# A two-layer attention and MLP backward on one Trainium2 core: dV stored in two halves, and two zero stores moved from the w1 backward to the dW1 chunks

## The chip, the core and the metric

The kernel runs on one core of one Trainium2 chip. The metric is the device time of one execution in microseconds (us), lower is better. A core has five engines that run their own instruction streams: PE (matrix products; "PEld" is the loading of its stationary operand), DVE (vector), ACT (scalar), POOL and SP. SP does nothing here but issue DMA transfers, in program order; POOL issues some as well. All transfers share the core's 16 DMA engines.

## The reference, cut to what matters

One token x of width 1024 goes through four residual layers: attention A, MLP B, then A and B again, with the same weights both times. The kernel returns the output and the gradients of everything.

```python
def _A_ref(x, k_cache, v_cache, wq, wo):        # 32 query heads, 4 kv heads, last W = 4096 keys
    q = (x @ wq) ...; p = softmax(q k^T * Dh**-0.5); o = p v
    return o @ wo
def _B_ref(x, w1, b1, w2):                       # F = 3584
    h = x @ w1 + b1;  act = h * tanh(softplus(h));  return act @ w2

x = x + A(layernorm(x));  x = x + B(layernorm(x))
x = x + A(layernorm(x));  x = x + B(layernorm(x))
...
out, vjp = jax.vjp(f, A_x, A_k_cache, A_v_cache, A_wq, A_wo, B_w1, B_b1, B_w2)
return (out, *vjp(grad_out))
```

The caches are 32768 keys long and only the last 4096 are used. So the gradients dK and dV (4 x 32768 x 128 in bf16, 33.5 MB each) are zero in seven eighths of their rows. These zeros have to be written too: 112 stores of 512 KB (the kernel calls them zero jobs), each from one zeroed tile `zt`. The last eighth of dK and of dV, 4 MB each, and the weight gradients dWq, dWo (8 MB each), dW1, dW2 (7 MB each) are sums of a few outer products and are computed at the end.

## The kernel before, in words

**The order of the work.** Attention forward (A1), MLP forward (B2), attention forward (A3), a pass that does the last MLP forward and backward at once (B4), attention backward of A3, a pass over w2 that finishes B4 forward and serves the backward of B2, the w1 backward of B2 (L798), attention backward of A1 (L817), and then the tail: all large gradients. The schedule is manual: each engine's instructions run in the order in which the Python code issues them.

**The zero stores** are used as filling for the DMA queues. `bg_zeros(n, after)` (L134) lets POOL copy one column of a tile `after`, so that POOL waits until that tile is there (a gate), and then POOL issues n zero stores. `zeros(n)` (L128) lets SP issue n of them, with no gate. The table `Z` (L1158) says how many go where: 85 go by POOL and 27 by SP.

**The w1 backward** (L788 to L815) streams w1 in 16 loads of 448 KB (L366) through a pool of six tiles. For each chunk, PE transposes 14 blocks (L196), DVE or ACT copies them back into the same tile (L146, L149), and PE does 14 small products with `dh` (L232). The load of a chunk is issued by SP when the products of the chunk six before it have freed its tile. `Z["W1m"]`, the tuple (2, 5, 8, 11, 13) in the kernel before, names the chunks at which a zero store is issued by POOL, gated on the chunk before (L793).

**The tail** is a list of jobs (L1288 to L1297), run one after the other. A job makes one chunk of a gradient: PE writes outer products into two PSUM tiles, ACT and DVE cast them to bf16 into an SBUF tile ("evacuation", `evac`, L143, which gives each piece to the engine with less work so far), and SP stores the chunk. The list is:

- 14 chunks of dW2, then 8 chunks of dW1 (`dw_tall` L1069, `dw_wide` L1084; stores at L1080 and L1099);
- 8 further chunks of dW1, each followed by one of the 8 chunks of dV (`dkv`, L1105);
- 16 chunks of dWo;
- 16 half chunks of dWq and 8 chunks of dK, two and one in turn (dWq is stored at L1101, every second half chunk, 1 MB).

The chunks of dW1, dW2 and dWo go to a ring of staging tiles: six in `wo_b`, six `st_o`, four in `V`, sixteen in `wq_b`. dWq goes to `wq_b` at fixed places. dV and later dK are gathered in the tile `K`, whose old contents are no longer needed. `late_prep` puts small preparations between the jobs, and after it `zeros(2)` is inserted into the list at positions 27 and 33 (L1294), which is among the dW1 and dV chunks. Zero jobs that are left at the end would be issued last (L1297); none are.

**The stores of dV and dK** are in `dkv`:

```python
if j % 4 == 3 and (j > 4 or half):
    hs = slice(4 * j - 12 if half else 0, 4 * j + 4)
    for g in range(G):
        nc.sync.dma_start(ov[:, g, hs, :], st[:, g, hs, :])
```

With `half` false, nothing is stored until the eighth chunk (j = 7), and then four stores of 1 MB go out, one for each kv head g. Chunk j fills the rows 4j to 4j+3 of each partition and head, so the first four chunks fill rows 0 to 15 and the others rows 16 to 31.

Of the kernel before, what the change touches and what calls it, by code (L numbers as in the profile page):

```python
# [23 lines left out]
def kernel(  # L24
# [40 lines left out]
    NW2 = TF // 2  # L65
# [62 lines left out]
    def zeros(n):  # L128
        for _ in range(min(n, len(zero_jobs))):
            nc.sync.dma_start(zero_jobs.pop(0), zt[:])  # L130
# [3 lines left out]
    def bg_zeros(n, after):  # L134

        if n:
            nc.gpsimd.tensor_copy(gate_t[:], after[:, 0:1])
        for _ in range(min(n, len(zero_jobs))):
            nc.gpsimd.dma_start(zero_jobs.pop(0), zt[:])  # L139
# [91 lines left out]
    def mm(out_ap, lhsT, rhs, start, stop, **kw):  # L231
        nc.tensor.matmul(out_ap, lhsT=lhsT, rhs=rhs, start=start, stop=stop, skip_group_check=True, **kw)  # L232
# [117 lines left out]
    def wo_load(c):  # L350
        if c < NR:
            w = wo_kept[c]
        else:
            w = strm.tile([P, 2, D], BF16, name="wo_c", tag="st")[:]
        nc.sync.dma_start(w, wo_v[c])
        return w
# [38 lines left out]
    area = {}  # L395
# [44 lines left out]
    def attn_fwd(x_col, lname, first):  # L440
# [30 lines left out]
        if not first:  # L471
            for c in range(NR, min(NO, NR + NB)):
                held[c] = wo_load(c)
            bg_zeros(Z["A3"], n_bf)
            for w in wq_t:
# [193 lines left out]
    def mlp_fwd(x_col, lname, g_bf):  # L669
# [5 lines left out]
        for i in range(2 * TD):  # L675
            t, hf = i // 2, i % 2
            w = w1_load(i)
            if i == 0:
                bg_zeros(Z["B2a"], x_col)
            if i == 4:  # L680
# [17 lines left out]
        sv["dact"] = dact  # L698
        x_new, wg = w2.rest(0, g_bf, x_col, f"x_{lname}", gbc, Z["B2"], last)
        return x_new, sv, wg  # L700
# [5 lines left out]
    def w1_block(b, hh):  # L706
        w = strm.tile([P, HT, CB], BF16, name="w1_b", tag="st")
        nc.sync.dma_start(w[:], w1_v[:, hh * HT:(hh + 1) * HT, b * CB:(b + 1) * CB])
        return w

    def mlp_turn(x_col, lname, wg, g_col, nxt):
# [22 lines left out]
        def lo0(b):  # L734
            return max(b - 1, 0) * FB

        def X(b, hh):
            wf = ws[b][hh][:].rearrange("p t f -> p (t f)")
            for k in range(2):
                xpose(*alt_blocks(wf[:, k * 1024:(k + 1) * 1024], 4), None, True)  # L740

        for b in range(NBK):
            if b:
                bg_zeros(Z["B4"][b], dh_bf[:, lo0(b):])
            ws[b] = [w1_block(b, hh) for hh in range(2)]
# [9 lines left out]
            if not b:  # L755
                bg_zeros(Z["B4"][b], m["y"])
            X(b, 0)
# [30 lines left out]
    def w1_T():  # L788
# [3 lines left out]
        ws[i] = w  # L792
        if i in Z["W1m"]:  # L793
            bg_zeros(1, ws[i - 1])
# [254 lines left out]
    def ev_out(out_ap, in_ap, f=1.0):  # L1049
        evac(out_ap, in_ap, 1.22 * f, 1.05 * f)  # L1050
# [10 lines left out]
    def out_banks():  # L1061

        if "pair" in pools:
            ts = [pools["pair"].tile([P, 1024], FP32, name="ops", tag="pair") for _ in range(2)]
            return [t[:, k * 512:(k + 1) * 512] for t in ts for k in range(2)], [(0, 2, ts[0][:]), (2, 2, ts[1][:])]
        bs = [psum1([P, 512], FP32, "ops") for _ in range(4)]
        return bs, [(k, 1, bs[k]) for k in range(4)]
# [37 lines left out]
    def dkv(x3, y3, x1, y1, out_t, half):  # L1105
        ov = out_t[0, :, Sk - W:, :].rearrange("g (p t) d -> p g t d", p=P)

        def chunk(j):
            st = kv["K"]
            bs, gs = out_banks()  # L1110
            for lay, (x, y) in enumerate(((x3, y3), (x1, y1))):
                for c in range(NC):
                    mm(bs[c], x[32 * c:32 * c + 32, j * P:(j + 1) * P],
                       y[32 * c:32 * c + 32, :, :].rearrange("p g d -> p (g d)"), lay == 0, lay == 1, tile_position=(32 * c, 0))
            for k, n, ap in gs:
                t0 = 4 * j + k
                ev_out(st[:, :, t0:t0 + n, :].rearrange("p g t d -> p t g d"), ap.rearrange("p (t g d) -> p t g d", t=n, g=G), n / 2)
# [5 lines that stand above are left out]
        jobs.extend([lambda j=j: chunk(j) for j in range(TJ)])  # L1123
# [31 lines left out]
        for _ in range(min(n, len(prep))):  # L1155
            prep.pop(0)()

    Z = dict(B2a=1, B2={0: 1, 4: 1, NW2 - 2: 3}, A3=14, B4=[2, 2, 2, 2, 2, 2, 5], A3c=6, A3d=28, B4w={1: 1, 4: 1, 7: 1, 10: 1, 12: 2}, W1=0, W1m=(2, 5, 8, 11, 13), A1c=3, A1d=23)  # L1158


    x1 = None
# [35 lines left out]
    x1, sA1 = attn_fwd(x0, "A1", True)  # L1197
# [51 lines left out]
    def r3(nm):  # L1249
        return area[nm].rearrange("p (g d) -> p g d", g=G)  # L1250
# [4 lines left out]
    def take(nm):  # L1255
        stage[nm] = jobs[:]
        del jobs[:]

    take("w")
    dkv(area["p3"], r3("do3"), sA1["p"], r3("do1"), out_3, False)  # L1260
    take("v")
    dw_tall("wo", HQ, out_5.rearrange("(c p t) d -> c p t d", p=P, t=2))
    take("o")
# [27 lines left out]
    weave(stage["q"], stage["k"], 2)  # L1291
    for at, f in zip((8, 11, 24, 27, 30, 40, 43, 46, 49, 51, 53), late_prep):
        jobs.insert(at, f)
    for at in (27, 33):  # L1294
        jobs.insert(at, lambda: zeros(2))
    run(1000)
    zeros(1000)  # L1297
# [31 lines left out]
```

## Time and profile before

| | |
|---|---|
| median of 11 runs | 444.97 us (440.87 to 448.15) |
| the profiled execution | 443.3 us, of which its span (first to last instruction) is 441.5 us |
| busy share of the span | PE 72%, ACT 50%, DVE 55%, POOL 15% |
| moved by DMA | 171.18 MB, 388 GB/s over the span |
| zero stores | 85 by POOL, 27 by SP, 512 KB each |
| w1 backward | about 262 to 290 us of the span |
| attention backward of A1 | about 290 to 326 us |
| tail | 326 us to the end |

How to read the profile: the page cuts the span into 40 equal slices and gives the busy share of each engine in tenths, the granted PE clock in tenths of full speed, the mean busy share of the 16 DMA engines, and the GB/s that they moved. A view by stretches gives the same for any stretch of time. A timeline lists instructions in order of time, and in square brackets how long the engine was idle just before and what ended that. A DMA has an issue time and a landing time; the view of DMA issues gives the time between the two.

### The profile page before, as it was taken

Reading aid. Unit: us, or ns where it says so; the run is one execution under the profiler, and the core shown is the slowest. Engines: PE = TensorE matmul, PEld = TensorE weight load, DVE = VectorE, ACT = ScalarE, POOL = GpSimd, SP = SyncE. Lnnn points to the kernel's source line nnn. Section 1 sums busy time; section 2 is a strip of 40 time slices with the busy share of each in tenths; the row PEclk is TensorE's granted clock in tenths of the full one; section 3 lists DMA queues with packets and bytes.
Section 4 is the critical chain, followed back from the end, with each engine's and each line's share of the span. In section 5 each row is a group of like instructions: output and inputs, shape, how many; then the busy total and the mean of one; then the engine's idle time right before and its main releaser. Section 6 shows DMA issues by size and latency. Waiting matters only on the chain.

```text
span 441.5 us, 11711 instructions
## 1 busy us (share of the span) xinstructions
PE 319.9 (72%) x5004; PEld 215.1 (49%) x5004; DVE 241.0 (55%) x494; ACT 219.3 (50%) x254; POOL 64.7 (15%) x168
## 2 busy tenths in 40 slices
PE   1565855597989989887995677787957588688830
PEld 0343525486376989875974676765421122211100
DVE  3134201196343766673547545464369889899930
ACT  1123100075143877867844333426047888798940
POOL 2000000011320322322333011214010010000000
PEclk9989555585888999999999559969965555555555
DMA  8999999999999999999999999999999986999997
GB/s 316 427 416 417 407 408 389 408 366 359 379 416 363 366 371 372 392 406 416 415 410 380 411 368 351 405 415 415 418 393 408 405 323 269 371 404 406 421 422 303
DMA packets 48720, 171.18 MB, mean 388 GB/s; under 512 B 4928, under 2 KB 12124, under 8 KB 44572
## 3 DMA queue, kind: packets, MB, share of 16 engines
q1 hardware_dynamic: 36208, 125.58, 72.3%
q0 software_dynamic: 12416, 44.84, 25.7%
q8 instruction: 39, 0.64, 0.6%
q14 instruction: 13, 0.11, 0.1%
q10 hardware_dynamic: 44, 0.01, 0.0%
HBM read 71.58 MB, written 98.84 MB: 386 GB/s over the span
## 4 chain that ended last, share of the span: by engine, by line
PE 24%; ACT 13%; DMA 11%; DVE 4%; issue 2%; POOL 1%; ACTq 0%; DVEq 0%; SPq 0%
DMA w_c<-in_B_w_dram 8%; PE tps L196 6%; PE ops L232 6%; PE acc L232 5%; ACT wq_b L149 3%; ACT K L149 3%; DMA out_dram<-wq_b 2%; ACT st_o L149 2%; PE sm L232 2%; ACT V L149 2%; ACT wo_b L149 2%; PE rw L995 1%; PE wps L155 1%; PE d L232 1%; PE tps L629 1%
## 5 line engine op out<-in xcount | busy, mean ns | idle before, releaser
L139 POOL DMA_DIRECT2D out_dram<-zt x85 | 45.8, 542 | 45.0 <-DMA out_dram<-zt 38.8
L232 PEld LDWEIGHTS <-w_c 128*128 128x128 bf16 x1120 | 37.4, 102 | 29.4 <-DMA w_c<-in_B_w_dram 23.2
L639 ACT COPY w_c<-tps 128x1024 bf16<-128x1024 bf16 x28 | 28.3, 1012 | 33.7 <-PE tps L629 26.3
L653 DVE CUSTOM_DVE_ANT_0 scr<-w_c,gbc 128x1024 bf16<-128x1024 bf16 x28 | 34.2, 1221 | 16.0 <-DMA w_c<-in_B_w_dram 14.8
L232 PE MATMUL ops<-V 2*128 2x512 bf16 (+1 forms) x160 | 33.4, 602 | 4.8 <-ACT V L149 1.2
L149 ACT CAST wq_b<-ops 128x1024 bf16<-128x1024 f32 (+1 forms) x33 | 35.9, 1128 | 1.9 <-PE ops L232 1.8
L146 DVE CAST wq_b<-ops 128x1024 bf16<-128x1024 f32 (+1 forms) x31 | 34.4, 1138 | 2.0 <-PE ops L232 1.8
L149 ACT COPY K<-tps 128x1024 bf16<-128x1024 bf16 x20 | 19.5, 1032 | 29.1 <-PE tps L196 29.0
L232 PEld LDWEIGHTS <-V 128*128 128x128 bf16 (+2 forms) x448 | 16.8, 102 | 33.7 <-issue 32.0
L232 PE MATMUL ops<-wo_b 2*128 2x512 bf16 x120 | 24.0, 569 | 9.8 <-ACT wq_b L149 2.7
L232 PE MATMUL acc<-a_pair,w_c 128*128 128x16 bf16 x448 | 15.9, 173 | 13.7 <-DMA w_c<-in_B_w_dram 13.7
L629 PE MATMUL tps<-ident_bf,w_c 128*128 128x128 bf16 x224 | 23.5, 270 | 0.7 <-DMA w_c<-in_B_w_dram 0.7
L149 ACT COPY w_b<-tps 128x1024 bf16<-128x1024 bf16 x20 | 19.5, 1015 | 5.3 <-PE tps L196 5.2
L232 PE MATMUL q<-wq_b,nA_pair 128*32 128x512 bf16 x128 | 10.6, 455 | 15.3 <-DMA wq_b<-in_A_wq_dram 15.3
L146 DVE COPY K<-tps 128x1024 bf16<-128x1024 bf16 x12 | 8.1, 690 | 24.0 <-PE tps L196 24.0
L248 DVE COPY yr<-acc 128x512 f32<-128x512 f32 x6 | 4.2, 692 | 30.9 <-PE acc L232 30.9
L232 PEld LDWEIGHTS <-wo_b 2*128 2x128 bf16 (+1 forms) x184 | 7.6, 101 | 27.2 <-issue 24.9
L146 DVE COPY w_c<-tps 128x1024 bf16<-128x1024 bf16 (+1 forms) x20 | 12.7, 650 | 14.2 <-PE tps L196 11.9
L149 ACT CAST K<-ops 128x1024 bf16<-128x1024 f32 x17 | 17.1, 1012 | 6.3 <-PE ops L232 5.5
L196 PE MATMUL tps<-ident_bf,K 128*128 128x128 bf16 x256 | 20.1, 240 | 0.2 <-ACT K L149 0.2
L146 DVE CAST K<-ops 128x1024 bf16<-128x1024 f32 x15 | 18.3, 1221 | 3.1 <-PE ops L232 2.7
L196 PE MATMUL tps<-ident_bf,w_c 128*128 128x128 bf16 x224 | 16.6, 231 | 4.7 <-DMA w_c<-in_B_w_dram 4.6
(326 smaller groups left out, 657.2 us busy)
## 6 DMA issues: line engine op xcount, KB each, us to landing
out_dram<-zt POOLq DMA_DIRECT2D x85, 512.0 KB, 10.4
w_c<-in_B_w_dram SPq DMA_DIRECT2D x32, 448.0 KB, 6.4
w_c<-in_B_w_dram SPq DMA_DIRECT2D x28, 512.0 KB, 8.5
out_dram<-zt SPq DMA_DIRECT2D x27, 512.0 KB, 10.6
wo_c<-in_A_wo_dram SPq DMA_DIRECT2D x24, 512.0 KB, 7.8
wq_b<-in_A_wq_dram SPq DMA_DIRECT2D x8, 1024.0 KB, 21.3
out_dram<-K SPq DMA_DIRECT2D x8, 1024.0 KB, 9.6
out_dram<-wq_b SPq DMA_DIRECT2D x8, 1024.0 KB, 10.3
```

Source lines behind the costliest of these rows:

```text
L139: nc.gpsimd.dma_start(zero_jobs.pop(0), zt[:])
L146: nc.vector.tensor_copy(out_ap, in_ap)
L149: nc.scalar.copy(out_ap, in_ap)
L155: nc.tensor.matmul(ps, lhsT=ident_bf[:], rhs=ident_bf[:, None, :].to_broadcast([P, 4, P]), start=True, stop=True, skip_group_check=True)
L196: nc.tensor.transpose(ps[:, b, :], ap, ident_bf[:])
L232: nc.tensor.matmul(out_ap, lhsT=lhsT, rhs=rhs, start=start, stop=stop, skip_group_check=True, **kw)
L248: nc.vector.tensor_copy(yr[:], bank[:])
L629: nc.tensor.transpose(self.ps[c][:, b, :], w[:, 1, b * P:(b + 1) * P], ident_bf[:])
L639: nc.scalar.copy(self.w[c][:, 1, :], self.ps.pop(c)[:].rearrange("p b c -> p (b c)"))
L653: nc.vector.tensor_tensor_reduce(out=scr[:], in0=w[:, 0, :], in1=gbc[:], scale=1.0, scalar=0.0, op0=ALU.mult, op1=ALU.add, accum_out=self. ...
L995: nc.tensor.transpose(ps[:, j, :], sp[:, j, :], ident_bf[:])
```

## The change

```diff
-    Z = dict(..., W1m=(2, 5, 8, 11, 13), ...)
+    Z = dict(..., W1m=(2, 8, 13), ...)
...
-    dkv(area["p3"], r3("do3"), sA1["p"], r3("do1"), out_3, False)
+    dkv(area["p3"], r3("do3"), sA1["p"], r3("do1"), out_3, True)
...
-    for at in (27, 33):
+    for at in (24, 27, 33):
         jobs.insert(at, lambda: zeros(2))
```

Three things are edited. The two zero stores at chunks 5 and 11 of the w1 backward, with their gates, are gone from POOL's program. A third pair of zero stores stands in SP's program among the dW1 chunks, so there are six in place of four; of the 14 dW1 stores from `wq_b`, the pairs now follow the 6th, the 7th and the 8th, where before they followed the 7th and the 9th. And dV is stored in two halves: four stores of 512 KB (16 rows of 256 bytes for each partition and head) after its fourth chunk, and four after its eighth; dK is stored as before. In SP's program the first half of dV follows the 10th of the 14 dW1 stores from `wq_b`, and the second half the 14th.

The number of zero stores stays 112: 83 by POOL and 29 by SP. The bytes moved are the same.

More of the change, by code (lines that the diff above doesn't have):

```diff
@@ L1156, in nextprep @@
             prep.pop(0)()
-    Z = dict(B2a=1, B2={0: 1, 4: 1, NW2 - 2: 3}, A3=14, B4=[2, 2, 2, 2, 2, 2, 5], A3c=6, A3d=28, B4w={1: 1, 4: 1, 7: 1, 10: 1, 12: 2}, W1=0, W1m=(2, 5, 8, 11, 13), A1c=3, A1d=23)
+    Z = dict(B2a=1, B2={0: 1, 4: 1, NW2 - 2: 3}, A3=14, B4=[2, 2, 2, 2, 2, 2, 5], A3c=6, A3d=28, B4w={1: 1, 4: 1, 7: 1, 10: 1, 12: 2}, W1=0, W1m=(2, 8, 13), A1c=3, A1d=23)
     x1 = None
```

## The prediction

> **What bounds the kernel now.** I read the page's slices first, then the view by stretches, then SP's timeline and its landing times for the end, and PE's and POOL's timelines for the w1 backward. From the page, the DMA share of the 40 slices and what was moved:
>
> ```profile
> DMA  8999999999999999999999999999999986999997
> GB/s 316 427 416 417 407 408 389 408 366 359 379 416 363 366 371 372 392 406 416 415 410 380 411 368 351 405 415 415 418 393 408 405 323 269 371 404 406 421 422 303
> ```
>
> The DMA engines are full in nearly every slice; the exceptions are the first, two slices around 353 to 375 us, and the last. No engine is full over the span (PE 72%). So time is to be won where DMA has a hole that later bytes could fill, or where bytes stand ahead of something that an engine waits for. The view by stretches, for the tail (start:end, its length, busy us of PE, PEld, DVE, ACT, POOL, PE clock, DMA share, GB/s):
>
> ```profile
> 328.00:356.00 28.00, 18.42 (x106) 4.41 (x104) 25.50 (x30) 23.09 (x23) 0.59 (x4) 0.50 1.01 401
> 356.00:364.00 8.00, 7.57 (x54) 2.59 (x49) 6.37 (x7) 7.15 (x7) 1.12 (x6) 0.50 0.75 294
> 364.00:380.00 16.00, 12.95 (x89) 4.29 (x83) 15.30 (x21) 13.76 (x14) 0.00 (x0) 0.50 0.71 287
> 380.00:402.00 22.00, 15.95 (x88) 3.69 (x89) 20.02 (x23) 18.94 (x21) 1.02 (x2) 0.50 1.01 405
> 402.00:425.00 23.00, 18.63 (x102) 4.02 (x95) 20.52 (x18) 19.93 (x22) 0.00 (x0) 0.50 1.02 416
> 425.00:441.50 16.50, 0.00 (x0) 0.00 (x0) 0.00 (x0) 0.28 (x1) 0.00 (x0) 0.50 0.83 345
> ```
>
> To see: the hole is 8 x 0.25 = 2.0 us and 16 x 0.29 = 4.6 us, 6.6 us in all. Through it and to 425 us DVE and ACT stay about 90% busy with the evacuations, and in their lists of waits no DMA stands: they wait for PE alone, shortly. So the tail has two clocks. The chain of evacuations runs from 326.6 to 425.3 us and sets when the last store, dK, can go; DMA sets what follows. SP's timeline of the tail, and the landing times of the last two kinds of store (issue to landing, us, the last number):
>
> ```profile
> 347.68 8.39 SPq L1099 DMA_DIRECT2D out_dram<-wq_b  x7
> 356.12 1.11 SPq L130 DMA_DIRECT2D out_dram<-zt  x2
> 360.04 2.80 SPq L1099 DMA_DIRECT2D out_dram<-wq_b  x2
> 362.89 1.11 SPq L130 DMA_DIRECT2D out_dram<-zt  x2
> 364.53 10.43 SPq L1099 DMA_DIRECT2D out_dram<-wq_b  x5
> 376.75 3.05 SPq L1121 DMA_DIRECT2D out_dram<-K  x4
> 425.31 4.20 SPq L1121 DMA_DIRECT2D out_dram<-K  x4
> ...
> out_dram<-wq_b SPq DMA_DIRECT2D x1, 1024.0 KB, 6.7
> out_dram<-K SPq DMA_DIRECT2D x4, 1024.0 KB, 9.6
> ```
>
> To see: the 4 MB of dV come at 376.75, after the hole. Its first store found the queue empty and landed in 3.9 us. The last store of dWq, of the same size, was issued at 423.76 and took 6.7 us: 2.8 us of other bytes were still ahead of it. For the w1 backward, PE's timeline, and after the "..." POOL's:
>
> ```profile
> 273.62 0.96 PE L196 MATMUL tps<-ident_bf,w_c 128*128 128x128 bf16 x14 [1.71 <-DMA w_c<-in_B_w_dram]
> 277.72 0.96 PE L196 MATMUL tps<-ident_bf,w_c 128*128 128x128 bf16 x14 [0.54 <-DMA w_c<-in_B_w_dram]
> 284.08 0.96 PE L196 MATMUL tps<-ident_bf,w_c 128*128 128x128 bf16 x14 [0.97 <-DMA w_c<-in_B_w_dram]
> 287.40 0.96 PE L196 MATMUL tps<-ident_bf,w_c 128*128 128x128 bf16 x14 [0.78 <-DMA w_c<-in_B_w_dram]
> ...
> 271.48 0.53 POOL L139 DMA_DIRECT2D out_dram<-zt  x1 [0.28 <-issue]
> 281.39 0.53 POOL L139 DMA_DIRECT2D out_dram<-zt  x1 [0.28 <-issue]
> ```
>
> To see: PE waits here for loads of w1, and the two zero stores shown, which compete with them, are the two that go.
>
> **Part 1, two zero stores less in the w1 backward.** Chunks that don't wait follow each other by 1.13 to 1.15 us. From chunk 6 (273.62) to chunk 15 (287.40) there are nine steps in 13.8 us, where 9 x 1.15 = 10.3 us would do: 3.4 us could go at most. By bytes: 1 MB at the 390 GB/s of 272 to 288 us is 2.7 us. The store of 271.48 lay wholly ahead of the last load, 1.35 us. That of 281.39 landed about 7.7 us later (the landing time of zero stores there), at 289.1, so some four fifths of it was served before 287.4: 1.1 us. Against this 2.4 us, the store of chunk 13 stays, and since chunk 13 is now reached sooner, it is issued sooner beside the same last loads. The price lies between 0 (the loads wait for their tiles, not for DMA) and 2.7 us; I take 1.9, near the upper end, since the waits name the loads and DMA is full. POOL's two gates and issues (0.19 and 0.53 us each) go as well, worth nothing: POOL stood idle 4.2 and 3.3 us before these gates.
>
> What follows is late by nothing new: from the layer norm at 290 us to the start of the tail at 326.6 the chain of waits names PE, DVE, ACT and POOL and no DMA, and the 23 zero stores that SP issues there wait only for each other. So 1.9 us earlier at 290 is 1.9 us earlier at 425.
>
> The DMA page of the Trainium skill ("DMA: Bandwidth & Descriptors", section "Queues, rings and completion order") says that each DMA engine takes turns between the queues that have work, a packet at a time. By that rule a zero store on POOL's queue takes every other turn from the loads until it is done, so both stores would have cost their full share, 2.7 us, where I take 1.9.
>
> **Part 2, two zero stores more in the tail.** 1 MB, 2.5 us of DMA at 416 GB/s. The pairs now stand after the stores issued at 354.01, 355.74 and 360.04, just before the first part of the hole (2.0 us, from 356 on). They fill it and leave 0.5 us. If part 1 brings less than its 2.7 us of DMA time, the hole is wider by the difference, relative to the evacuations, since DMA comes to it with less work. SP pays two issues of about 0.5 us, at a place where it waits up to 2.7 us for the next evacuation. In the scheduled program each DMA that SP issues waits for the landing of its eighth predecessor; eight of 512 KB are 10 us, and landings here take 2.4 to 5.6 us, so this stops nobody.
>
> **Part 3, dV in two halves.** The fourth dV chunk is evacuated by 365.9 us (DVE's cast of 364.67, 1.23 us), so 2 MB, 5.0 us, are issued from about 366 on, over a hole of 4.6 us. They leave 0.4 us. This adds a wait: SP holds for that evacuation. Behind it stand the last four dW1 stores (366.87 us and later), late by one or two us at most, and their tiles are next written by dWq after 397 us. Two more waits change: chunks 1 and 5 of dK now wait for the first and the second half of dV, where the first waited for all. dV's last 1 MB landed at 389.9 (378.57 + 11.3), the first dK cast is at 399.3: 9 us of cover. In the scheduled program the casts of dV's chunks 5 to 8, which write `K` while the first half is read from it, wait for PE alone. Four more DMAs are issued, 0.4 to 0.6 us of SP each, beside its waits. Rows of 4 KB in place of 8 KB: the zero stores have rows of 4 KB too, and 308 to 324 us, nothing but zero stores nearly, moved 414 to 423 GB/s, as the 1 MB stores of dK did (421). So nothing.
>
> Here the same page (section "Bandwidth") speaks against the change: transfers should be batched to 1 MiB or more. By its fit (section "Anatomy of one DMA", 2.0 us fixed for each transfer issued by POOL), an estimate for four more is up to 8 us if nothing overlapped. The queued 512 KB stores at 414 to 423 GB/s show that here it does.
>
> **The sum.** DMA is relieved by 6.6 of hole less 2.5 of zeros, 4.1 us, more than the 2.8 us of backlog at the last dWq store. So at 423.76 the queue is empty, and the evacuations bound the end. Then only dWq's last 1 MB and dK's 4 MB are to move after 425 us: 5.24 MB, where 16.5 us x 345 GB/s = 5.69 MB moved before. 0.45 MB at 421 GB/s is 1.1 us. By landings, the last dWq store would land 2.8 us earlier, but dK's first store can't land before 425.31 + 3.9 = 429.2 and its fourth, 2.5 us for each, before 436.7, against 439.0 (428.2 + 10.8): at most 2.3 us. I take 1.3, nearer the count of bytes. So 1.9 + 1.3 = 3.2 us. The profiled execution took 443.3 us (span 441.5, and 1.8 around it): 440.1. The median of the runs is 1.7 above that execution, so of a median **445.0 - 3.2 = 441.8 us**. About 0.5%, 2.2 us, is what a measurement of this kernel can tell from no change.
>
> **Rivals.**
> - *Only one of the two gains.* For it: the zeros of 266.3 and 283.8 us stay, and the largest PE wait (1.71 us at 273.62) comes from a load issued at 267.4, before the first removed store could disturb it. Or the tail's backlog is smaller in other executions than in this one. Against: DMA is full through the stretch, and the 6.7 us landing is plain. 445.0 less 1.3 to 1.9: about 443.4.
> - *The edit is hidden.* w1's loads run at the rate at which PE frees tiles, and the end is set by the evacuations and dK's own 10 us, so nothing moves: 445.0. Against it speak the nine steps of 13.8 us. The half store not acting at all is excluded by the scheduled program.
> - *Slower: the moved megabyte is paid at the end.* Place: the hole. If the two zeros bring nothing in the w1 backward, and the hole is already filled (the evacuations come later or DMA comes with more backlog, as the 40 slices can't exclude for other executions), then 2.5 us of zeros are in the queue that the last dK store stands in: 445.0 + 2.5 = 447.5. It decides from the point where the gain at 290 us and the hole together are under 2.5 us. Against: 6.6 us of hole.
>
> **How the numbers follow.** Both gains: 0.54, with 0.5 to 2.7 for part 1 and 0.9 to 2.3 for the tail, a gain of 2.2 to 4.8 (440.2 to 442.8). One gain: 0.23. Hidden: 0.10. Paid at the end: 0.13. So faster by over 0.5%: 0.54; within: 0.33; slower: 0.13. The range takes in the first three cases and 1 us on either side for the scatter of a median whose single runs lie 7 us apart: 439.0 to 446.0.
>
> **What would show it.** Part 1: the last chunk's transposes near 285.5 us instead of 287.4, and PE's waits for `w_c` after 275 us down from 2.6 (0.54, 0.27, 0.97, 0.78) to below 1. Part 2 and 3: a DMA share near 1.0 from 356 to 380 us, four `K` stores near 365, and no DMA among the waits of ACT and DVE. The tail: dWq's last landing near 4 us, not 6.7, and the span's end 14.9 us after dK's first store, not 16.2. Wrong would make it: w1 loads that land no sooner; a cast of `K` that waits for a store; or a hole that comes back after 380 us because the evacuations, not DMA, fed the tail all along.

## The result, and the profile after

The changed kernel took 438.53 us (median of 12 runs, 434.83 to 441.39) where the kernel before took 444.80 us (47 runs): ratio 0.986, 95% interval 0.983 to 0.989, a gain of 6.3 us. Forecast were 441.8 us, a gain of 3.2, and a range from 439.0. So the sign and both mechanisms were as forecast, and the gain was about twice as large. The change was then measured three more times (below): 0.9934, 0.9939 and 0.9853. The four average 0.9897, 4.6 us.

The profiled execution of the changed kernel took 438.51 us, its span is 436.7. From the page, the same two lines as those of before:

```profile
DMA  8999999999999999999999999999999999999978
GB/s 317 421 419 416 407 408 385 408 383 384 383 415 378 359 369 362 389 407 418 415 410 381 411 369 378 348 403 413 416 376 406 404 399 406 402 400 409 418 323 360
```

To see: the hole in the 33rd and 34th slice is gone, and a smaller one has come just before the end. The view by stretches of the tail (start:end, length, busy us of PE, PEld, DVE, ACT, POOL, PE clock, DMA share, GB/s):

```profile
356.00:364.00 8.00, 7.28 (x47) 2.04 (x47) 7.00 (x8) 7.88 (x8) 1.12 (x6) 0.50 1.02 400
364.00:380.00 16.00, 12.36 (x84) 4.19 (x81) 14.87 (x21) 13.58 (x14) 0.00 (x0) 0.50 1.02 405
380.00:402.00 22.00, 16.58 (x89) 3.80 (x90) 20.61 (x23) 19.00 (x21) 1.02 (x2) 0.50 1.01 402
402.00:421.00 19.00, 15.93 (x90) 3.70 (x89) 17.88 (x17) 16.64 (x18) 0.00 (x0) 0.50 0.94 387
421.00:436.70 15.70, 0.88 (x6) 0.00 (x0) 0.85 (x1) 1.93 (x2) 0.00 (x0) 0.50 0.85 351
```

The share from 356 to 380 us was 0.75 and 0.71; it is 1.02. From 402 us on it falls below 1: the queue runs empty there, and it did not before. SP's timeline of the same stretch, dV's halves and dK:

```profile
364.21 4.33 SPq L1121 DMA_DIRECT2D out_dram<-K  x4
375.02 3.54 SPq L1121 DMA_DIRECT2D out_dram<-K  x4
423.46 3.80 SPq L1121 DMA_DIRECT2D out_dram<-K  x4
```

dK's first store is issued at 423.46 us (425.31 before), and SP sees the last landing at 435.9 (440.7 before). Both are the start of the first of SP's three closing drains, before which SP waits for dK's stores (10.6 us in the kernel before). The first line is the kernel before, the second the changed one:

```profile
L1324 SPq DRAIN  x3: 7/7/7, 440.7 to 441.0; - x3
L1324 SPq DRAIN  x3: 7/7/7, 435.9 to 436.2; - x3
```

So 4.8 us are gained, 1.85 of them before dK's first store and 2.95 after it. The chain of evacuations between them has the same length, 98.6 us here and 98.7 before, and ACT and DVE wait for no DMA in it.

The 1.85 us are less than they look. PE's timeline of the w1 backward, the chunks that wait for their loads:

```profile
272.18 0.96 PE L196 MATMUL tps<-ident_bf,w_c 128*128 128x128 bf16 x14 [1.62 <-DMA w_c<-in_B_w_dram]
278.29 0.96 PE L196 MATMUL tps<-ident_bf,w_c 128*128 128x128 bf16 x14 [0.26 <-DMA w_c<-in_B_w_dram]
282.09 0.96 PE L196 MATMUL tps<-ident_bf,w_c 128*128 128x128 bf16 x14 [0.79 <-DMA w_c<-in_B_w_dram]
285.80 0.95 PE L196 MATMUL tps<-ident_bf,w_c 128*128 128x128 bf16 x14 [1.28 <-DMA w_c<-in_B_w_dram]
```

Chunk 15 starts at 285.80, 1.6 us sooner; but the first product of the stage had come at 265.51 and not 266.87, 1.36 us sooner, from stages that the edit doesn't touch. One pair of profiles can't price this part.

### The profile page after: what moved, and what is told of

It reads as the page before. It is cut to its first block, busy times and chain, and to the rows that moved or that the text cites. A ratio compares the mean times of both kernels' runs of the same rounds, so it can differ in the third digit from the quotient of the medians.

```text
span 436.7 us, 11719 instructions
## 1 busy us (share of the span) xinstructions
PE 319.6 (73%) x5004; PEld 215.3 (49%) x5004; DVE 241.0 (55%) x494; ACT 219.3 (50%) x254; POOL 62.7 (14%) x164
## 4 chain that ended last, share of the span: by engine, by line
PE 24%; ACT 15%; DMA 9%; DVE 4%; issue 2%; POOL 1%; ACTq 0%; DVEq 0%; SPq 0%
DMA w_c<-in_B_w_dram 8%; PE tps L196 6%; PE ops L232 6%; PE acc L232 5%; ACT wq_b L149 4%; ACT K L149 3%; ACT st_o L149 2%; PE sm L232 2%; ACT V L149 2%; ACT wo_b L149 2%; PE rw L995 1%; PE wps L155 1%; DMA out_dram<-wo_b 1%; PE d L232 1%; PE tps L629 1%
## 5 line engine op out<-in xcount | busy, mean ns | idle before, releaser
L139 POOL DMA_DIRECT2D out_dram<-zt x83 | 44.2, 535 | 45.3 <-DMA out_dram<-zt 39.7
L639 ACT COPY w_c<-tps 128x1024 bf16<-128x1024 bf16 x28 | 28.3, 1012 | 32.4 <-PE tps L629 24.5
L146 DVE COPY w_c<-tps 128x1024 bf16<-128x1024 bf16 (+1 forms) x20 | 12.7, 650 | 13.8 <-PE tps L196 8.7
## 6 DMA issues: line engine op xcount, KB each, us to landing
out_dram<-zt POOLq DMA_DIRECT2D x83, 512.0 KB, 10.6
```

Source lines behind the costliest of these rows:

```text
L146: nc.vector.tensor_copy(out_ap, in_ap)
L639: nc.scalar.copy(self.w[c][:, 1, :], self.ps.pop(c)[:].rearrange("p b c -> p (b c)"))
```

## The experiments

The theory after the result: the change is a sum of two parts, the zero stores out of the w1 backward (some 1 to 2 us) and the end of the tail (2.9 us by the two profiles). The rivals: the moved zeros bring most of it; or something beyond the parts does; and for the end of the tail, that it was dV's halves as such and not the empty queue.

**Each part alone, and more of it.** Four kernels on one chip. Halves only:

```diff
-    dkv(area["p3"], r3("do3"), sA1["p"], r3("do1"), out_3, False)
+    dkv(area["p3"], r3("do3"), sA1["p"], r3("do1"), out_3, True)
```

> Only the two halves of dV, all zero stores where they were. Theory (the end of the tail is most of the gain): the last 4 MB of dK find an empty queue, the span ends 13 to 14 us after dK's first store as in the changed kernel (13.2) and not 16.2; ratio 0.990 to 0.994 (2.7 to 4.5 us). Rival (the moved zeros bring most of it): ratio 0.996 to 1.000.

The two zero stores moved, dV in one piece:

```diff
-    W1m=(2, 5, 8, 11, 13)
+    W1m=(2, 8, 13)
-    for at in (27, 33):
+    for at in (24, 27, 33):
```

> Only the two zero stores moved from the w1 backward into the dW1 chunks; dV in one piece. Theory: the w1 backward gains 0.3 to 1.9 us, and the zeros fill part of the hole and nothing is taken from the end, where the dK stores still stand behind a full queue (16 us): ratio 0.995 to 1.000. Rival (the moved zeros bring most of it): 0.987 to 0.992.

The changed kernel, with dK in halves too:

```diff
-    dkv(sA3["ds"], r3("q3"), sA1["ds"], r3("q1"), out_2, False)
+    dkv(sA3["ds"], r3("q3"), sA1["ds"], r3("q1"), out_2, True)
```

> The changed kernel with dK in two halves as well. Theory (after the change the end is bound by the evacuations and by the last 4 MB of dK, 10 us of DMA): 2 MB less after the last evacuation, but the queue has only about 2.4 us of idle time between 402 and 423.5 us to take them earlier, so 2 to 2.5 us less than the changed kernel: ratio 0.980 to 0.983. Rival (DMA is already full to the end, bytes set it): as the changed kernel, 0.986.

The two zero stores out of the w1 backward into the last attention backward, with the tail as before:

```diff
-    W1m=(2, 5, 8, 11, 13), ... A1d=23
+    W1m=(2, 8, 13), ... A1d=25
```

> The two zero stores leave the w1 backward and go to the 23 zero stores that SP issues in the last attention backward; the tail is as before. This measures part 1 alone. Prediction's own price: 1.9 us, ratio 0.996. Rival from the two traces (chunk 15 comes 1.6 us earlier, but 1.35 of these were there before the stage began): 0.3 us, ratio 0.999. If the zeros are worth more in most executions than in the profiled ones: 0.993 or less.

Measured: halves only 0.9958 (0.9924 to 0.9991), zeros moved 0.9959 (0.9923 to 0.9995), dK in halves too 0.9894 (0.9839 to 0.9948; 0.980 to 0.983 was expected), w1 part alone 0.9949 (0.9912 to 0.9985). So each of the two parts gives about 2 us, neither gives most, and the w1 backward part is near the 1.9 us that the prediction gave it. Both theories had a share wrong: the halves' whole time moved less than their profile (1.9 us against 2.9), the w1 part more than the 0.3 us of the two traces.

The profiles separate the two cleanly. From dK's first store to the last landing it takes 15.4 us in the kernel before, 15.3 with the zeros moved, 15.5 with the w1 part alone, and 12.6 with the halves alone. Where the 2.9 us lie is seen in the last microseconds of DMA. The view by stretches of the kernel before:

```profile
437.00:438.00 1.00, 0.00 (x0) 0.00 (x0) 0.00 (x0) 0.00 (x0) 0.00 (x0) 0.50 1.02 426
438.00:438.50 0.50, 0.00 (x0) 0.00 (x0) 0.00 (x0) 0.00 (x0) 0.00 (x0) 0.50 0.71 295
438.50:439.00 0.50, 0.00 (x0) 0.00 (x0) 0.00 (x0) 0.00 (x0) 0.00 (x0) 0.50 0.12 49
439.00:439.50 0.50, 0.00 (x0) 0.00 (x0) 0.00 (x0) 0.00 (x0) 0.00 (x0) 0.50 0.04 16
439.50:440.00 0.50, 0.00 (x0) 0.00 (x0) 0.00 (x0) 0.00 (x0) 0.00 (x0) 0.50 0.04 16
```

and of the changed one:

```profile
434.00:435.00 1.00, 0.00 (x0) 0.00 (x0) 0.00 (x0) 0.00 (x0) 0.00 (x0) 0.50 1.06 442
435.00:435.50 0.50, 0.00 (x0) 0.00 (x0) 0.00 (x0) 0.00 (x0) 0.00 (x0) 0.50 0.37 148
435.50:436.00 0.50, 0.00 (x0) 0.00 (x0) 0.00 (x0) 0.00 (x0) 0.00 (x0) 0.50 0.00 0
```

To see: before, after the bulk of the data there is a trail of about 1.5 us at a share of 0.04 to 0.12, which of sixteen engines is one or two. In the changed kernel the bulk breaks off at once. The bulk itself ends about 1.2 us sooner after dK's first store (11.8 against 12.9 us in quarter-microsecond steps), which is what the count of bytes had given. The trail is 1.25 us shorter (0.25 against 1.5). The remaining half microsecond lies between the last bytes and SP's notice of the landing; no run explains it.

The version with dK in halves was a try for a faster kernel. Counted from the first store of dK's second half, its bulk ends after 9.4 us, 2.4 sooner than in the changed kernel, as expected; but its queue is full from 402 to 425 us again, and the trail is the longest of these:

```profile
402.00:425.00 23.00, 17.66 (x94) 3.80 (x91) 19.63 (x17) 19.47 (x21) 0.00 (x0) 0.50 1.02 417
...
433.00:434.00 1.00, 0.00 (x0) 0.00 (x0) 0.00 (x0) 0.00 (x0) 0.00 (x0) 0.50 0.84 336
434.00:435.00 1.00, 0.00 (x0) 0.00 (x0) 0.00 (x0) 0.00 (x0) 0.00 (x0) 0.50 0.13 53
435.00:436.00 1.00, 0.00 (x0) 0.00 (x0) 0.00 (x0) 0.00 (x0) 0.00 (x0) 0.50 0.07 29
```

It lands 12.7 us after that store, no sooner than the changed kernel (12.4).

**Again, and a late engine made on purpose.** The changed kernel and the kernel before, unaltered, and each with one more store among the dWo stores:

```diff
+    lag_to = out_2[0, 0, 0:ZR, :].rearrange("(p r) d -> p (r d)", p=P)[0:127, 0:256]
+    jobs.insert(64, lambda: nc.sync.dma_start(lag_to, zt[0:127, 0:256]))
```

> The changed kernel unaltered, measured again beside the kernel before, and a second profile of it. If the two parts simply add (w1 backward about 2.0 us by the single edits, end of the tail 2.9 us by the profiles), the ratio is 0.987 to 0.991. If they reinforce each other, 0.986 or less again.

> The kernel before unaltered, for a second profile: which stages scatter between executions. Expected: evacuation chain (first wo_b cast to dK's first store) 98.7 us as in all six profiles so far; from dK's first store to the landing of its last one 15.3 to 15.4 us; the w1 backward, first product to last, anywhere from 22 to 25 us.

> The kernel before with one more store of zeros over zeros, 127 partitions x 512 bytes = 65 KB, among the dWo stores; 127 is prime, so it may be served by one DMA engine instead of sixteen, some 2.5 us of that engine. Theory (after the bulk of dK one late DMA engine sets the landing, because the queue never ran empty to let it catch up): from dK's first store to the last landing 15.3 us grow by up to 3 us, with a longer trail at a share of about 0.06. Rival (the end is set by bytes, 0.04% more): 15.3 to 15.5 us as before.

> The same 65 KB store in the changed kernel. Theory: the queue runs empty before the last stores, the late engine catches up there, and from dK's first store to the last landing it stays 12.4 to 12.6 us. Rival: as in the kernel before, the same growth.

The changed kernel: 0.9934 (0.9899 to 0.9969), a gain of 2.9 us, less than the first time and less than either of the two expected. The second profile of the kernel before repeats the first where it counts: evacuations 98.7 us, 15.4 us from dK's first store to the landing, trail 1.5 us.

The store on few engines told less than hoped. In the kernel before, the time from dK's first store to the landing grew from 15.4 to 18.1 us, but as bulk and not as trail: it held up the whole queue. The view by stretches of that kernel:

```profile
404.00:406.00 2.00, 1.93 (x12) 0.41 (x8) 1.94 (x3) 2.00 (x3) 0.00 (x0) 0.50 1.01 404
406.00:408.00 2.00, 1.68 (x14) 0.39 (x10) 1.93 (x3) 1.23 (x2) 0.00 (x0) 0.50 0.12 29
408.00:410.00 2.00, 1.88 (x8) 0.31 (x6) 2.00 (x2) 2.00 (x3) 0.00 (x0) 0.50 0.72 280
```

For two microseconds one or two engines worked (a share of 0.12) and the others had nothing; the 29 GB/s are 58 KB in that time, nearly the 63.5 KB of the store. Meanwhile SP's next store took 7.5 us to issue. In the changed kernel the landing grew by 0.9 us to 13.4, nearly all of it trail (1.0 us in place of 0.25), which neither the theory nor the rival had. So in these two executions one slow share of a transfer cost the whole queue in the first kernel and made a trail in the second; but as a test of the first kernel's trail it is inconclusive. The Trainium skill ("DMA: Bandwidth & Descriptors", section "Why a DMA increments its semaphore by 16 and not by 1") says that a transfer is spread over the largest number of engines, up to 16, that divides the outer dimension of both sides, so that one of 127 partitions issued by SP goes to a single engine; the share of 0.12 agrees in kind, though it is nearer to two engines.

**The whole once more, and all five zeros out of the w1 backward.**

> The changed kernel unaltered, a third time. Two measurements gave 6.3 us (4.9 to 7.5) and 2.9 us (1.4 to 4.5). The sum of the parts, 2.9 us at the end of the tail and 1 to 2 us from the w1 backward, is 4 to 5 us: ratio 0.989 to 0.991. Rival (something that the parts don't hold adds 2 us or more): 0.986 or less.

```diff
-    W1m=(2, 5, 8, 11, 13), ... A1d=23
+    W1m=(), ... A1d=28
```

> The kernel before with none of the five zero stores in the w1 backward; all five go to the zero stores that SP issues in the last attention backward. Price of a zero store there, from the profiles (about 0.5 to 0.9 us each) 2.5 to 4.5 us in all, ratio 0.990 to 0.994; PE's waits for w1 loads fall from 3.6 to 5.1 us to below 1.5. Rival (the price is nothing, the scatter makes it): 0.998 to 1.002. From dK's first store to the last landing 15.4 us, as before.

and in the changed kernel:

```diff
-    W1m=(2, 8, 13), ... A1d=23
+    W1m=(), ... A1d=26
```

> The changed kernel, with the three other zero stores of the w1 backward moved as well, to SP in the last attention backward. A try for a faster version: the evacuations start 1.5 to 2.5 us sooner, and DMA has about 2.4 us of holes left between 402 and 423 us to take what is displaced. Theory: 1 to 2.4 us less than the changed kernel. Rival (DMA is full from there to the end, and the late engine's trail of 1.3 us comes back): the same as the changed kernel.

The changed kernel: 0.9939 (0.9905 to 0.9973), 2.7 us, again less than either expected. With no zeros in the w1 backward, and the tail as before: 0.9926 (0.9894 to 0.9958), 3.3 us, and 15.2 us after dK's first store, as expected. By the whole times that is 0.7 us for each of the five zero stores, 1.3 us for two; the two alone measured 1.9.

The profiles can't settle this price. From the first product of the w1 backward to the last it takes 19.3 us there, 21.3 to 22.8 us with three zeros (nine profiles of all sections) and 21.8 to 25.6 us with five (six). But the clock granted to PE in this stage ran from 0.78 to 1.00, between executions of the same instructions too. The stage to the end of the last product, in the second profile of the kernel before and in the second one of the halves, whose program is the same up to the tail (columns as in the views above):

```profile
268.09:290.38 22.29, 18.10 (x420) 17.22 (x420) 10.34 (x16) 10.02 (x12) 3.12 (x9) 1.00 1.02 386
266.73:292.82 26.09, 21.22 (x420) 20.58 (x420) 10.34 (x16) 10.01 (x12) 3.11 (x9) 0.80 0.99 370
```

To see: the same 420 instructions of PE keep it busy for 18.1 us at a granted clock of 1.00 and for 21.2 us at 0.80. Sorted by it, at 0.99 or 1.00 the stage took 21.8 to 22.3 us with five zeros (three profiles), 21.5 and 22.1 us with three and 19.3 us with none; at 0.78 to 0.93 it took 24.5 to 25.6 us with five (three), 21.3 to 22.8 us with three (seven) and 21.8 us with none (the next kernel). Between the means, two zero stores are worth 0.3 us at the full clock and about 3 us below it, from too few profiles to call either a price.

PE's waits for w1 loads were 1.7 us with no zeros, against 3.6 to 5.1 with five; less than 1.5 was expected.

The same edit in the changed kernel gave 0.9918 (0.9887 to 0.9948), not distinguishable from the changed kernel beside it. Its w1 backward took 21.8 us in the profile, its queue is full from 402 to 424 us and its trail is 2.3 us; from dK's first store to the landing 15.7 us. So the rival of that run came true in what it said of the end: DMA full, the trail back, no gain that can be told. That time gained at 290 us was given back there is not shown: this profile's evacuations began at 325.5 us, no sooner than in the changed kernel's (324.8 to 329.5).

**An empty queue alone.** The kernel before, with six stores of dWo left out:

```diff
-            nc.sync.dma_start(out_v[c], st[:])
+            if nm != "wo" or c not in range(4, 10):
+                nc.sync.dma_start(out_v[c], st[:])
```

> The kernel before, with six of the sixteen stores of dWo left out (3 MB, so that part of dWo is not written), which come between 383 and 400 us; dV and dK are stored as before. The queue is then empty well before the last stores. Theory (one late DMA engine, which catches up when the queue is empty): from dK's first store to the last landing 12.4 to 12.6 us, trail 0.25 us, as in the changed kernel. Rival (the halves of dV themselves do it, or the trail belongs to dK's stores): the bulk ends 11.7 us after dK's first store but the trail of 1.25 to 1.5 us stays, 13.7 us or more.

dV leaves in one piece here, dK is stored as ever, and the time from dK's first store to the landing is 12.7 us, in one execution. The DMA share is 0.87 from 400 to 425 us, where it was full in the kernel before. The end of its DMA:

```profile
442.00:443.00 1.00, 0.00 (x0) 0.00 (x0) 0.00 (x0) 0.00 (x0) 0.00 (x0) 0.50 0.99 410
443.00:443.50 0.50, 0.00 (x0) 0.00 (x0) 0.00 (x0) 0.00 (x0) 0.00 (x0) 0.50 0.63 262
443.50:444.00 0.50, 0.00 (x0) 0.00 (x0) 0.00 (x0) 0.00 (x0) 0.00 (x0) 0.50 0.01 0
```

The trail is gone (0.25 us) and the bulk ends 11.6 us after dK's first store. So the 2.9 us (here 2.7) belong to a queue that ran empty before the last stores, whatever emptied it; the halves are only the means. The kernel before this one is the converse: it has the halves and a full queue, and takes 15.7 us.

**The whole and its parts on one chip.**

> The changed kernel, a fourth time, beside its parts. If the parts add up: the sum of the gains of the next two kernels, 4 to 5 us. If they hide each other: 2.7 to 3 us. If they reinforce each other: over 6 us.

> Only the two halves of dV, again. 2.9 us by the profiles (15.4 to 12.5 us after dK's first store); 1.9 us measured the first time.

> Only the two zero stores out of the w1 backward, again. 1.2 us by the mean start of the evacuations less the scatter before the stage; 2.3 us measured the first time.

Measured 0.9853 (0.981 to 0.990), halves 0.994 (0.9903 to 0.9976), w1 part 0.9967 (0.9934 to 1.000). Here the whole, 6.5 us (4.6 to 8.4), is more than its parts, 2.7 and 1.5, though not clear of the scatter of the three; in the two repeats before it was 2.9 and 2.7 us, less than the parts' mean sum of 4.2. Over all measurements: halves 0.995 (2.3 us), w1 part 0.996 (1.9), whole 0.990 (4.6). On average the parts add up, and the whole scatters from measurement to measurement by more than its intervals say. The averages also mix chips: both parts, each time, and the fourth measurement of the whole were taken on one chip, the second and the third on two others, and for the first the chip is not on record.

## Why the prediction was wrong

**Part 1, two zeros less in the w1 backward: right within the scatter, 1.9 us forecast.** Measured alone 2.3 and 1.5 us, mean 1.9, with intervals of 1.5 us on either side, so that the agreement to a tenth is chance; by the five zeros 1.3. That the zeros delay the loads is borne out by PE's waits with none of them, 1.7 and 1.8 us against 3.6 to 5.1 with five. Its sign in the profile was wrong: PE's waits after the sixth chunk were to fall from 2.6 us to below 1, and are 2.8 us (0.26, 0.43, 0.79, 1.28) in the profiled execution. That the last chunk came at 285.8 us, near the forecast 285.5, was owed to the stages before. In single profiles this stage scatters by nearly 4 us between executions of the same instructions (21.8 to 25.6), with the granted clock for a large part, more than the effect; the prediction read the one trace at a clock of 0.99 and gave the clock no term.

**Part 2, two zeros more in the tail: right, nothing.** They lie in the hole, whose first part (356 to 364 us) has a share of 1.02. With the zeros moved and no halves, the landing stays 15.3 us after dK's first store.

**Part 3, dV in two halves: right in its mechanism.** The first half was issued at 364.21 (forecast about 365), the hole from 364 to 380 us filled, no cast waits for a store, and the 512 KB stores cost nothing: 405 GB/s in that stretch. The rule of the Trainium skill on batching to 1 MiB ("DMA: Bandwidth & Descriptors", section "Bandwidth") again doesn't show in a queue that always has the next transfer.

**The sum: the term that failed is the end of the tail.** The prediction wrote "I take 1.3, nearer the count of bytes", between 1.1 by bytes and 2.3 by landings. By the profiles it measured 2.9 to 3.0 us (15.4 to 12.4), above both, and 2.3 us by the whole times of the halves alone. Two errors made it. The count of bytes was right for the bulk (1.2 us), but the last landing is not the end of the bulk: a trail of one or two late engines followed, 1.5 us, which stands in the last rows of the kernel before (0.12, then 0.04) and which the prediction put at nothing. And the upper bound by landings put the end before at 439.0 (428.2 + 10.8): the 10.8 us are those of dK's third store (427.00 to about 437.8), the view gives none for the fourth, and SP saw the end only at 440.7. What it had right: the queue ran empty (a share of 0.94 from 402 to 421 us), and dWq's store of 418.29 landed in 3.9 us, forecast near 4. (A hole after 380 us stands among its signs of being wrong, though its own sum needs the queue empty at 423.76; the hole came, and the gain with it.) With 1.9 + 2.9 = 4.8 us the sum would have said 440.2 us, and the four measurements average 4.6 us. A slip beside it: the ranges of the two terms, 0.5 to 2.7 and 0.9 to 2.3, make a gain of 1.4 to 5.0 us and not the 2.2 to 4.8 that the prediction wrote.

**What is left of the first measurement.** 6.3 us is 1.5 more than this sum. The four measurements of the same change, 6.3, 2.9, 2.7 and 6.5 us, disagree beyond their intervals. Their profiles agree in the tail: evacuations 98.62 to 98.66 us, 12.4 to 12.5 us from dK's first store to the landing. They differ in stages that the change doesn't touch: the w1 backward's first product comes at 265.5 to 268.2 us, and from its last to the first evacuation it takes 36.5 to 39.1 us. The second of these goes with the granted clock: 39.05 us at 0.84 with PE busy for 32.0 us (third measurement), 37.26 at 0.87 (first), 36.52 at 0.93 with PE busy for 29.5 us (second and fourth); the kernel before had 37.40 at 0.87.

Over whole runs the clock goes with the time too. Among the runs of the kernel before in each of the last three measurements, 0.01 more of mean granted clock went with 1.4 to 2.3 us less. The changed kernel's runs had a mean clock of 0.750 in the first and the fourth measurement and 0.743 in the other two, the kernel before 0.742 to 0.745 in the last three. By that slope, an estimate, the clock would account for about 1 us of the fourth gain and for half a microsecond missing in the second; the larger part of the disagreement stays open, and no run varied the clock or the chip on purpose.

**The rivals.** "Only one of the two gains" and "hidden" fell with the two parts measured alone. "The moved megabyte is paid at the end" did not occur with this change; in the kernel that moved three more zeros, where the queue was full to the end, the last landing came 3.3 us later after dK's first store and no gain could be told.

## What to carry to other kernels

Where DMA is full nearly everywhere, look for the hole, and ask whether bytes that are ready before it are issued after it: a store cut in two and moved ahead by one half was worth about half of the gain here, with no byte less. Price the end of a kernel by the last landing and not by the bytes, and look at the last microseconds of DMA share for a trail. And before a pair of profiles is read for a microsecond, see how much the stages scatter that the edit doesn't touch, and compare the clock that was granted in them.

## What the runs showed of the hardware

The trail at the end depends on whether the queue ran empty shortly before. In the seven executions where it did (the changed kernel four times, the halves twice, the six stores left out), the bulk breaks off within 0.25 us. Where the queue had last had a hole between 356 and 380 us (the kernel before twice, the zeros moved, the w1 part twice, no zeros in the w1 backward) the trail is 1.25 to 1.75 us, and in the two kernels where it had been full through the whole tail (dK in halves too, the changed kernel without zeros in the w1 backward) 2.3 to 2.5 us. The reading that fits is that one or two of the sixteen engines fall behind while the queue is full and catch up when it is empty; the views don't tell the engines apart. Shown is the dependence on the empty queue, by the run with six stores left out; what makes them late is not. A candidate is the loading of instructions, which in the kernel before came in two packets of 16 KB between 380 and 440 us, 0.2% of 16 engines' time there, 1.9 us of one engine. The changed kernel has the same two packets there, and no run varied them.

A transfer that is served by few engines holds up more than itself: 63.5 KB in 127 rows left the other engines idle for two microseconds, and from dK's first store to the last landing it took 2.7 us more, in one execution.

The clock granted to PE differs between executions of the same instructions: in the w1 backward it was 0.78 to 1.00, and PE was busy there for 18.1 us at 1.00 and for 21.2 us at 0.80.
